# The second product of the second MLP's last 1536 tokens by seven block products, gates of a pass first

## The chip, the cores and the metric

The kernel runs on one core of a Trainium2 chip. The metric is device time in microseconds (us) of one execution, the median of several runs. One execution was also recorded by the hardware profiler; all rows below come from it. In the rows PE is the matmul engine TensorE, PEld its weight loads, DVE is VectorE, ACT is ScalarE, POOL is GpSimd, and SP is the engine that issues nearly all DMAs. L284 is line 284 of the kernel. A releaser is the instruction whose end let a waiting one start.

## What is computed

Random-feature attention over 4 batches of 576 tokens is followed by two MLPs over all 2304 tokens, in float32. Cut to what matters:

```
x = attention(q, k, v, omega)                 # 2304 tokens x 512
h = x @ w_in;   g = max(h, 0) + alpha * min(h, 0)
x = g @ w_out                                 # first MLP, 512 -> 2048 -> 512
h = x @ w_in2
g = where(h >= 1, h, where(h <= -1, 0, (h + 1) ** 2 / 4))
out = g @ w_out2                              # second MLP, 512 -> 2048 -> 512
```

## The kernel before

**Numbers as pairs.** Each float32 operand of an MLP product is held as a high part (rounded to the format that TensorE takes) and a low part (the rest). A product is three matmuls into the same sum: high by high, high by low, low by high (`mm3`, L284 to L286). Splitting an operand costs one ACT instruction for the high part (`hi_of`, L268) and one subtraction on DVE or POOL for the low part (`lo_of`, L277 to L279).

**Stages.** Attention and the first MLP's first three groups of 512 tokens run interleaved: 48 *units* (3 groups by 16 blocks of 128 hidden features). The first of them starts at about 56 us, the 48th ends at about 390 us. Then come four *passes* of 768 tokens: pass 0 is the rest of the first MLP, passes 1 to 3 are the whole second MLP. A pass has 8 *steps* (s = 8 p + j), and step j makes the hidden features of two blocks of 128.

**First product of a step.** It is done by seven block products instead of eight (Strassen's scheme in Winograd's form): input and weights are cut into 2 by 2 blocks, sums of blocks are made ahead, and product i (0 to 6) takes 6 matmuls of 128x384 (`product`). Products 4 and 6 are copied out by ACT (`kept_copy`, L1093) and products 2 and 3 are then added on top of them in the same PSUM bank (`CHAINS`). DVE forms four *corners* from the results (`shared_sum`, `added_corner`, `last_corner`: L1103, L1112, L943), each 128 features by 384 tokens. `corner` applies the gate (for the second MLP a clamp on DVE, a square on ACT, a maximum on DVE: L1143 to L1145) and splits the result into high and low part in one of four places (`out_g_slots`).

**Second product.** It is plain: per step two blocks by six rows of 128 tokens by three matmuls of 128x512, summed over the pass in six PSUM banks (`piece`). The pieces of step s - 1 are put between the seven products of step s by the list `PIECES`, so that DVE and ACT have a whole step of about 15.6 us to make one step's gates. At the end of a pass `store` copies six banks out and sends them to `out`.

**Weights.** The second MLP's weights come in while the first MLP and pass 0 run: `second_weights` starts block f at unit 16 + 3.4 f, `convert` turns the raw words into float32, `second_parts` makes and splits the block sums of the first product's weights, `keep_out` splits the second product's weights as they are. All go to DRAM through three staging tiles (`stage_slots`, tiles `w_keep`), and each step reloads them (`load_set`, `load_out`).

**Order.** The order of every engine is fixed when the kernel is built. `Plan` picks, one after the other, the stream that can start first by estimated durations, ranks and free places, so a changed stream also moves others. Every engine then works off its own list in order, and a wait holds up all that stands behind it.

Of the kernel before, what the change touches and what calls it, by code (L numbers as in the profile page):

```python
# [176 lines left out]
def favor_attention_two_mlps(  # L177
# [20 lines left out]
    nc = tc.nc  # L198
# [24 lines left out]
    W2S = 4, 5  # L223
    PACE = 34
# [134 lines left out]
    def keep_out(f, w):  # L359
        yield ev("w", 1, f, 1)  # L360
        j, u = divmod(f, 2)
        yield from keep(kept[1, j, 3 + u], w, (1, j, 3 + u))
        plan.put(w_slots[1], slot_of[1, f, 1])
# [534 lines left out]
    ORDER = [0, 5, 6, 3, 4, 1, 2]  # L898
    CHAINS = {2: 4, 3: 6}
# [8 lines left out]
    set_slots = [*part_slots, Tokens([0])]  # L908
# [6 lines left out]
    for m in range(2):  # L915
        for j in range(NJ2):
            for k in range(5):
                n = DM if k != 2 else 3 * DM // 2
                kept[m, j, k] = dram.tile([P, 2, n], F32, tag=f"kept{m}_{j}_{k}", name="w_kept")
    for j in range(NJ2):  # L920
        kept[0, j, 5] = dram.tile([P, 2, DM], F32, tag=f"odd{j}", name="w_kept")

# [77 lines left out]
    def load_set(s, k):  # L1000
        p, j, m = step(s)
        n = len(w_sets[k]) * DM // 2
        if s:
            yield ev("set", s - 1, k)
        if k < 2:
            yield ev("part", NU - 1, k)
        yield ev("second")
        yield ev("stored", m, j, k)
        if k == 2:
            yield ev("stored", m, j, 6)  # L1010
        t = yield set_slots[k]
        if k < 2:
            both = part_tile(t, "w_set")
        else:
            both = second[0].tile([P, 2, n], F32R, tag="w2", name="w_set")
        yield _dma(P * n * 8, lambda: nc.sync.dma_start(both.bitcast(F32), kept[m, j, k]))
        w_of[s, k] = both[:, 0, :], both[:, 1, :], t
        done("set", s, k)

    def load_out():  # L1020
        yield ev("g", NU - 1)
        for s in range(STEPS):
            p, j, m = step(s)
            for u in (1, 0):
                yield ev("stored", m, j, 3 + u)
                t = yield g_slots
                both = moe_p.tile([P, 2, DM], F32R, tag=t, name="w_out") if t[0] == "g" else part_tile(t, "w_out")
                out_of[s, u] = both[:, 0, :], both[:, 1, :], t
                plan.add(load(both.bitcast(F32), kept[m, j, 3 + u], ("out part", s, u)), 0)

    def inputs(p):
# [17 lines left out]
        engine = ("dve2",) if p else ("pool",)  # L1049
# [22 lines left out]
    def split_input(p, i, src):  # L1072
        yield x_slots[i]
        pool = second[0]
        hi = pool.tile([P, K2, GH], F32R, tag=f"sh{i}", name="x_hi")
        lo = pool.tile([P, K2, GH], F32R, tag=f"sl{i}", name="x_lo")
        yield hi_of(hi, src, 0)
        yield lo_of(lo, src, hi, ("dve2",) if p else ("pool",))
        x_of[p, i] = hi, lo
        done("xi", p, i)  # L1080
# [55 lines left out]

    def corner(s, q, h, key):
        p, j, m = step(s)
        u, half_ = divmod(q, 2)
        yield t_slots  # L1140
        t = temp("t")
        if m:
            yield _dve_fast(GH, lambda: nc.vector.tensor_scalar(t, h, -1.0, 1.0, ALU.max, ALU.min))  # L1143
            yield _act(GH, lambda: nc.scalar.activation(t, t, AF.Square, bias=half[:, 0:1], scale=0.5), 50)  # L1144
            yield _dve_two(GH, lambda: nc.vector.tensor_tensor(h, h, t, ALU.max))  # L1145
# [24 lines left out]
    def second_mlp():  # L1170
        yield ev("first hidden")
        banks = {}
        for s in range(STEPS + 1):
            pieces = second_project(s - 1) if s else iter(())
            p, j, _ = step(s)
            for i in range(2):
                done("unit", NU + 2 * s + i)
            for i, more in zip(ORDER, PIECES if s > NJ2 else FIRST_PIECES):
                if s < STEPS:
                    chain = CHAINS.get(i)  # L1180
                    k = place[i][0]
                    yield ev("set", s, k)
                    yield ev("xi", p, i)
                    if chain is None:
                        tag = yield h_banks
                        banks[i] = bank(tag), tag
                    else:
                        yield ev(f"e{chain}", s)
                        banks[i] = banks.pop(chain)
                    b, tag = banks[i] if i in (4, 6) else banks.pop(i)  # L1190
                    o = b[:, :GH]
                    yield product(s, i, o, chain is None)
                    if i in (0, 4, 6):
                        plan.add(kept_copy(s, f"e{i}", o, tag), URGENT)
                    if i == 5:
                        plan.add(shared_sum(s, o, tag), URGENT)
                        plan.add(last_corner(s), URGENT)
                        plan.add(shared_sum_used(s), URGENT)
                    if i in (1, 2, 3):
                        plan.add(added_corner(s, i - 1, o, tag), URGENT)  # L1200
                    if i == max(w_sets[k], key=ORDER.index):
                        plan.put(set_slots[k], w_of[s, k][2])
                    if j == NJ2 - 1:
                        plan.put(x_slots[i], 0)
                for _ in range(more):
                    yield from next(pieces, ())

    def spare():
        for j in range(NJ2):
            for k in (0, 1, 2, 3, 4, 6):  # L1210
                yield ev("kept", 1, j, k)
        i = yield stage_slots
# [48 lines left out]
    def piece(s, p, j, u, r):  # L1261
# [11 lines left out]
        yield _pe(mm3_ns(DM), lambda: mm3(y, gh, gl, hi, lo, first, last))  # L1273
        if last:
            plan.add(store(p - 1, r, y, tag, tokens), URGENT)
        if r % (NR // 2) == NR // 2 - 1:
            plan.put(out_g_slots[q], 0)
        if r == NR - 1:
            plan.put(g_slots, t_out)

    def store(p, r, y, tag, tokens):
# [18 lines left out]
        if c < B * SM:  # L1300
            b, t = divmod(c, SM)
            at = b * S + t
            yield _dma(P * DM * 4, lambda: nc.sync.dma_start(rows((at, at + P)), dst))
            return
        for i in range(P // SL):
            at = ((c - B * SM) // SL + i) * S + SM
            yield "dma", 300, lambda: nc.sync.dma_start(rows((at, at + SL)), dst[i * SL : (i + 1) * SL])

# [87 lines left out]
    for s in range(STEPS):  # L1396
        for k in range(3):
            plan.add(load_set(s, k), 0)
    for p in range(1 + NG):
        plan.add(inputs(p), URGENT + 1 + p)  # L1400
# [51 lines left out]
```

## Time and profile before

| | |
|---|---|
| median of 3 runs | 905.27 us (904.07 to 907.48) |
| profiled execution, its own time | 903.9 us |
| its span, first to last instruction | 902.1 us |
| PE busy | 887.8 us (98%) |
| DVE, ACT, POOL busy | 622.9, 457.9, 281.0 us |
| DMA moved | 221.36 MB, mean 245 GB/s |
| granted TensorE clock | 1.0 (2.4 GHz) in all 40 slices |

A busy figure is time in which an engine had work in flight. Matmuls overlap: the duration of one (391 ns for 128x512) is longer than the distance between the starts of two neighbours, and it is the distance that counts for the time of a long run of them. The span's stretches, cut at the first matmul of each pass, are: 145 to 390 us first MLP (with the attention's later part), then pass 0, 1, 2, 3.

### The profile page before, as it was taken

Reading aid. Unit: us, or ns where it says so; the run is one execution under the profiler, and the core shown is the slowest. Engines: PE = TensorE matmul, PEld = TensorE weight load, DVE = VectorE, ACT = ScalarE, POOL = GpSimd, SP = SyncE. Lnnn points to the kernel's source line nnn. Section 1 sums busy time; section 2 is a strip of 40 time slices with the busy share of each in tenths; the row PEclk is TensorE's granted clock in tenths of the full one; section 3 lists DMA queues with packets and bytes.
Section 4 is the critical chain, followed back from the end, with each engine's and each line's share of the span. In section 5 each row is a group of like instructions: output and inputs, shape, how many; then the busy total and the mean of one; then the engine's idle time right before and its main releaser. Section 6 shows DMA issues by size and latency. Waiting matters only on the chain.

```text
span 902.1 us, 16293 instructions
## 1 busy us (share of the span) xinstructions
PE 887.8 (98%) x6017; PEld 757.8 (84%) x6017; DVE 622.9 (69%) x1180; ACT 457.9 (51%) x998; POOL 281.0 (31%) x257
## 2 busy tenths in 40 slices
PE   8999999999999999999999999999999999999997
PEld 7677777777777788889999999999999989999996
DVE  5997767765556844597887999566855559565553
ACT  6886777555666422453444565343533335443333
POOL 1766666565758764931120022000000000000000
PEclk9999999999999999999999999999999999999999
DMA  8967765588988899989999879864665655664532
GB/s 215 240 198 226 209 232 191 175 266 297 312 298 290 293 326 344 330 322 322 308 340 323 291 263 321 289 207 167 216 240 187 198 172 202 223 213 158 206 111 94
DMA packets 84432, 221.36 MB, mean 245 GB/s; under 512 B 26752, under 2 KB 32512, under 8 KB 84352
## 3 DMA queue, kind: packets, MB, share of 16 engines
q1 hardware_dynamic: 84272, 220.27, 72.5%
q8 instruction: 48, 0.79, 0.3%
q14 instruction: 32, 0.26, 0.1%
q10 hardware_dynamic: 80, 0.03, 0.0%
HBM read 165.22 MB, written 55.05 MB: 244 GB/s over the span
## 4 chain that ended last, share of the span: by engine, by line
PE 89%; DVE 3%; DMA 2%; ACT 2%; issue 1%; POOL 1%; SPq 1%; DVEq 0%; POOLq 0%; ACTq 0%
PE h L284 13%; PE h L286 13%; PE h L285 13%; PE y L284 11%; PE y L285 11%; PE y L286 11%; PE a L286 3%; PE a L285 3%; PE a L284 3%; PE a L602 2%; PE a L465 2%; PE a L539 1%; PE a L568 1%; DMA w_set<-w_kept 1%; DVE nm L432 1%
## 5 line engine op out<-in xcount | busy, mean ns | idle before, releaser
L284 PE MATMUL h<-x_hi,w_set 128*128 128x384 f32 x448 | 151.4, 338 | 0.8 <-DMA w_set<-w_kept 0.5
L286 PE MATMUL h<-x_hi,w_set 128*128 128x384 f32 x448 | 150.9, 337 | 0.0
L285 PE MATMUL h<-x_lo,w_set 128*128 128x384 f32 x448 | 150.6, 336 | 0.0
L327 POOL TENSOR_TENSOR w<-w,raw 128x512 uint32<-128x512 uint32 x64 | 90.0, 1414 | 188.3 <-DVE w L326 143.2
L1144 ACT ACTIVATE t<-t,half 128x384 f32<-128x384 f32 x96 | 58.9, 613 | 91.5 <-DVE t L1143 91.1
L284 PEld LDWEIGHTS h<-x_hi,w_set 128*128 128x128 f32 x448 | 84.2, 188 | 9.4 <-DVE w_keep L278 0.9
L285 PEld LDWEIGHTS h<-x_lo,w_set 128*128 128x128 f32 x448 | 84.1, 188 | 7.5
L268 ACT ACTIVATE g<-c 128x384 fp32r<-128x384 f32 x96 | 50.4, 525 | 67.8 <-DVE c L1145 36.3
L286 PEld LDWEIGHTS h<-x_hi,w_set 128*128 128x128 f32 x448 | 84.1, 188 | 0.0
L284 PE MATMUL y<-g,w_parts 128*128 128x512 f32 x192 | 78.2, 407 | 0.6 <-ACT kf L443 0.6
L284 PE MATMUL h<-x_hi,w_parts 128*128 128x512 f32 x192 | 78.7, 410 | 0.0
L286 PE MATMUL h<-x_hi,w_parts 128*128 128x512 f32 x192 | 75.4, 393 | 0.9 <-POOL w_parts L279 0.8
L1093 ACT COPY e<-h 128x384 f32<-128x384 f32 x96 | 45.4, 473 | 59.2 <-PE h L286 58.4
L286 PE MATMUL y<-w_out,g 128*128 128x512 f32 x192 | 75.3, 392 | 0.0
L284 PE MATMUL y<-w_out,g 128*128 128x512 f32 x192 | 75.2, 392 | 0.0
L285 PE MATMUL y<-w_out,g 128*128 128x512 f32 x192 | 75.1, 391 | 0.0
L285 PE MATMUL y<-g,w_parts 128*128 128x512 f32 x192 | 75.1, 391 | 0.0
L286 PE MATMUL y<-g,w_parts 128*128 128x512 f32 x192 | 75.0, 391 | 0.0
L285 PE MATMUL h<-x_lo,w_parts 128*128 128x512 f32 x192 | 75.0, 391 | 0.0
L279 POOL TENSOR_TENSOR w_parts<-w,w_parts 128x512 fp32r<-128x512 f32 x48 | 62.8, 1316 | 34.3 <-ACT w_parts L268 27.9
L278 DVE TENSOR_TENSOR g<-c,g 128x384 fp32r<-128x384 f32 x96 | 54.6, 568 | 21.6 <-ACT g L268 21.3
L812 DVE TENSOR_SCALAR t<-h,alpha_sb 128x512 f32<-128x512 f32 x48 | 35.9, 748 | 47.1 <-PE h L286 47.0
(167 smaller groups left out, 2011.9 us busy)
## 6 DMA issues: line engine op xcount, KB each, us to landing
w_set<-w_kept SPq DMA_DIRECT2D x64, 512.0 KB, 4.6
w_out<-w_kept SPq DMA_DIRECT2D x64, 512.0 KB, 5.0
w_kept<-w_keep SPq DMA_DIRECT2D x56, 512.0 KB, 6.2
raw<-w SPq DMA_DIRECT2D x48, 512.0 KB, 5.9
w_parts<-w_kept SPq DMA_DIRECT2D x48, 512.0 KB, 5.3
w_set<-w_kept SPq DMA_DIRECT2D x32, 768.0 KB, 4.4
w_kept<-w_parts SPq DMA_DIRECT2D x32, 512.0 KB, 4.3
kq<-kq SPq DMA_DIRECT2D x15, 576.0 KB, 5.5
```

Of the source, the lines that this page charges most:

```text
L268: ops = [_act(n, lambda: nc.scalar.activation(hi, src, AF.Copy))]
L278: "dve2": _dve_two(n, lambda: nc.vector.tensor_tensor(*args), bias),
L279: "pool": _pool(n, lambda: nc.gpsimd.tensor_tensor(*args)),
L284: nc.tensor.matmul(out_, wh, mh, start=first, stop=False, skip_group_check=more)
L285: nc.tensor.matmul(out_, wh, ml, start=False, stop=False, skip_group_check=more)
L286: nc.tensor.matmul(out_, wl, mh, start=False, stop=last, skip_group_check=more)
L327: yield _pool(n, lambda: nc.gpsimd.tensor_tensor(d, d, low, ALU.add))
L465: nc.tensor.matmul(o, x[rows, c], om[rows, :], start=True, stop=True)
L602: nc.tensor.matmul(o[r], weights[i], moving[i], start=True, stop=True)
L812: yield _dve(SM + 57, lambda: nc.vector.tensor_scalar(t, h, 0.0, a, ALU.min, ALU.mult))
L1093: yield _act(GH, lambda: nc.scalar.copy(e, src))
L1144: yield _act(GH, lambda: nc.scalar.activation(t, t, AF.Square, bias=half[:, 0:1], scale=0.5), 50)
```

## The change

For passes 2 and 3 (steps from `PLAIN` = 16 on) the second product is also done by seven block products. Each pass is put into two halves: first all eight steps of the first product with all their gates, kept as 32 float32 tiles in SBUF places that have fallen free (`open_units`), then 7 by 8 block products (`second_products`) of 9 matmuls of 128x256, one product index after the other, each summed over the eight j in two banks. The token-side block sums are made by `gate_sums` on DVE or POOL, the operands are split by `operands`, up to four ahead, and `out_sums` forms the output corners. The weight-side sums are made once by `out_parts`, eight blocks per pair of f, so twice the bytes go to DRAM; `second_weights` starts at unit 12. The gate of passes 1 to 3 becomes two ACT instructions and one on DVE. Loads of passes 2 and 3 go through one ring of tiles (`late_loads`), and the first product's order in steps after 16 is `LATER_ORDER`. Pass 0 and pass 1 keep the plain second product.

```diff
-            yield ev("unit", NF + PACE * f // 10)
+            yield ev("unit", W2_FROM + PACE * f // 10)
...
-            if a:
-                plan.add(keep_out(f, w), NU + f)
...
+            if a and f % 2:
+                plan.add(out_parts(f // 2), NU + f)
+
+    def out_parts(j):
...
+        yield either(h, "tensor_tensor", (t1, b12, b11, ALU.subtract), off_way())
+        yield either(h, "tensor_tensor", (t2, b22, t1, ALU.subtract), off_way())
+        plan.add(keep_halves(sa.rearrange("p a n -> p (a n)"), ((j, 4), (j, 5))), rank)
+        yield either(h, "tensor_tensor", (t3, b22, b12, ALU.subtract), off_way())
+        yield either(h, "tensor_tensor", (t4, b21, t2, ALU.subtract), off_way())
+        plan.add(keep_halves(sb.rearrange("p a n -> p (a n)"), ((j, 6), (j, 3))), rank)
...
+    def keep_halves(src, keys):
+        i = yield stage_slots
...
+        yield hi_of(hi, src, 600)
+        yield lo_of(lo, src, hi, off_way())
...
+    LATER_ORDER = [0, 6, 4, 5, 3, 2, 1]
+    OUT_ORDER = [0, 4, 5, 6, 2, 3, 1]
+    OUT_CHAINS = {2: 4, 3: 6, 1: 0}
+    PLAIN = 2 * (NF // 2)
...
-        engine = ("dve2",) if p else ("pool",)
+        engine = ("dve2",) if p else ("dve2", "pool")
...
+    def gate(t, h, to):
+        yield _act(GH, lambda: nc.scalar.activation(t, h, AF.Relu, bias=half[:, 0:1], scale=0.5), 90)
+        yield _act(GH, lambda: nc.scalar.activation(t, t, AF.Square))
+        yield _dve_two(GH, lambda: nc.vector.scalar_tensor_tensor(to, h, 1.0, t, ALU.max, ALU.min))
...
+            if j == 0 and p > 2:
+                yield from second_products(p - 1)
+            pieces = second_project(s - 1) if 0 < s <= PLAIN else iter(())
...
+            order = ORDER if s <= PLAIN else LATER_ORDER
+            more = [0] * 7 if s > PLAIN else PIECES if s > NJ2 else FIRST_PIECES
...
+        yield from second_products(NG)
...
+        yield either(GH, "tensor_tensor", (a21, a21, a22, ALU.add), both)
+        done("first sum", s)
...
+    def operand(p, i, j, slot):
...
+        yield hi_of(hi, src)
+        yield lo_of(lo, src, hi, ("dve2",))
...
+                def products():
+                    for c, o in enumerate(os):
+                        r = slice(c * P, (c + 1) * P)
+                        mm3(o, hi[:, r], lo[:, r], w_hi, w_lo, chain is None and j == 0 and c != 1, j == NJ2 - 1, True)
```

On TensorE in a step of pass 2 or 3, before: `h` is a first product, `y` a sum of the second product, `g` the gates as weights, `w_out` the streamed weights.

```order
L285 MATMUL y_7725<-w_out,g_4276 128x512
L286 MATMUL y_7725<-w_out,g_4276 128x512
L284 MATMUL h_8540<-x_hi,w_set 128x384
L285 MATMUL h_8540<-x_lo,w_set 128x384
L286 MATMUL h_8540<-x_hi,w_set 128x384
```

After, at the end of the gates of pass 3, where the last first product meets the first block product:

```order
L286 MATMUL h_9874<-x_lo,w_set 128x384
L287 MATMUL h_9874<-x_hi,w_set 128x384
L285 MATMUL a_9885<-w_out,g_4352 128x256
L286 MATMUL a_9885<-w_out,g_4352 128x256
L287 MATMUL a_9885<-w_out,g_4352 128x256
```

Pieces of 128x512 no longer stand between the first products: 42 first-product matmuls per step follow each other in the gate half, and 504 of 128x256 in the product half.

On DVE in one step of pass 3, before (`u`, `e`, `c` are the sums that make the corners, `t` the gate's clamp, `g` the low parts):

```order
L1103 TENSOR_TENSOR u<-h_9091,e_9090 128x384
L278 TENSOR_TENSOR g_4275<-c_9067,g_4275 128x384
L943 TENSOR_TENSOR e_9122<-e_9122,u 128x384
L1112 TENSOR_TENSOR c_9141<-h_9115,u 128x384
L1143 TENSOR_SCALAR t<-c_9141 128x384
L1145 TENSOR_TENSOR c_9141<-c_9141,t 128x384
L278 TENSOR_TENSOR g_4276<-c_9141,g_4276 128x384
```

After, the first whole step of pass 3 (`gates` and `x` are places of kept gates, L995 a sum of them):

```order
L1236 TENSOR_TENSOR u<-y_9259,e_9237 128x384
L995 TENSOR_TENSOR e_9248<-e_9248,u 128x384
L1245 TENSOR_TENSOR c_9279<-y_9238,u 128x384
L995 TENSOR_TENSOR e_9248<-e_9248,e_9258 128x384
L1245 TENSOR_TENSOR c_9288<-a_9249,u 128x384
L1245 TENSOR_TENSOR c_9301<-y_9289,e_9237 128x384
L1273 SCALAR_TENSOR_TENSOR gates<-c_9279,gates 128x384
L1273 SCALAR_TENSOR_TENSOR gates<-e_9248,gates 128x384
L1273 SCALAR_TENSOR_TENSOR gates<-c_9288,gates 128x384
L995 TENSOR_TENSOR gates<-gates 128x384
L1273 SCALAR_TENSOR_TENSOR gates<-c_9301,gates 128x384
L995 TENSOR_TENSOR x<-gates 128x384
```

These 12 instructions are the whole step; before, a step had 18. The low parts (L279) have moved behind the last gate of the pass, two of the four sums per step as well. From one `u` to the next DVE has 12 to 14 instructions in the gate halves, ACT 11 to 13 (three copies, eight for the gates, at times a high part).

On POOL near the end of its list, before (`w` is a converted weight, `w_keep` a low part on its way to DRAM):

```order
L279 TENSOR_TENSOR x_lo<-x,x_hi 128x768 x2
L327 TENSOR_TENSOR w<-w,raw 128x512
L279 TENSOR_TENSOR w_keep<-w,w_keep 128x512
L327 TENSOR_TENSOR w<-w,raw 128x512 x20
```

After, where its conversions of the second MLP's weights near their end:

```order
L328 TENSOR_TENSOR w<-w,raw 128x512 x4
L996 TENSOR_TENSOR w_sum<-w 128x256
L996 TENSOR_TENSOR w_sum<-w,w_sum 128x256
L280 TENSOR_TENSOR w_keep<-w,w_keep 128x2x256 x2
L280 TENSOR_TENSOR w_keep<-w_sum,w_keep 128x2x256
L996 TENSOR_TENSOR w_sum<-w 128x256
```

POOL takes sums and low parts of the second product's weights between the conversions, and gives the eleven sums and low parts of pass 0's input (`x_lo`, `x_sum`, `x`, 128x768) to DVE. Over its whole list it gains 23 sums of 128x256 and 13 low parts of 128x512. ACT gains 15 high parts of 128x512 for these weights (one more is on DVE), and the stores of this product's weights to DRAM change from 16 of 512 KB to 64 of 256 KB.

## Rows read from the trace of the kernel before

**Rows 1.** The page's first part: busy us, share of span, instructions.

```profile
span 902.1 us, 16293 instructions
PE 887.8 (98%) x6017; PEld 757.8 (84%) x6017; DVE 622.9 (69%) x1180; ACT 457.9 (51%) x998; POOL 281.0 (31%) x257
```

**Rows 2.** Waits of PE, longest first: us in total, times, longest.

```profile
PE a L602 <- ACT kf L443: 1.7, 1, 1.7
```

**Rows 3.** Stretches: length; busy PE, PEld, DVE, ACT, POOL (x); clock, DMA share, GB/s.

```profile
145.00:390.00 245.00, 241.76 (x1792) 189.70 (x1792) 149.70 (x248) 124.80 (x283) 163.70 (x151) 1.00 0.84 287
390.00:514.20 124.20, 123.44 (x697) 114.04 (x696) 107.04 (x207) 57.40 (x109) 18.79 (x13) 1.00 0.92 322
514.20:638.90 124.70, 124.70 (x638) 113.31 (x637) 97.67 (x194) 59.49 (x114) 12.65 (x7) 1.00 0.71 249
638.90:763.80 124.90, 124.90 (x626) 112.91 (x625) 80.33 (x160) 50.74 (x98) 0.00 (x0) 1.00 0.57 198
763.80:902.10 138.30, 133.24 (x661) 119.34 (x659) 74.45 (x153) 53.49 (x104) 0.00 (x0) 1.00 0.50 169
```

**Rows 4.** Timeline of PE at the start of pass 2: start us, us, instruction.

```profile
638.88 0.34 PE L284 MATMUL h<-x_hi,w_set 128*128 128x384 f32 x1
...
640.99 0.39 PE L284 MATMUL y<-w_out,g 128*128 128x512 f32 x1
...
643.40 0.39 PE L284 MATMUL y<-w_out,g 128*128 128x512 f32 x1
...
645.45 0.34 PE L284 MATMUL h<-x_hi,w_set 128*128 128x384 f32 x1
```

**Rows 5.** Timeline of PE in pass 0: three matmuls of 128x256, and what follows.

```profile
450.95 0.27 PE L284 MATMUL a<-g,w_out 128*128 128x256 f32 x1
451.06 0.28 PE L285 MATMUL a<-g,w_out 128*128 128x256 f32 x1
...
451.30 0.34 PE L284 MATMUL h<-x_hi,w_set 128*128 128x384 f32 x1
```

**Rows 6.** Timeline of PE and PEld: twelve filling matmuls of 128x256 at 50 us.

```profile
49.97 1.69 PE L1337 MATMUL h<-warm_w 128*128 128x256 f32 x12
49.97 1.48 PEld L1337 LDWEIGHTS h<-warm_w 128*128 128x128 f32 x12
```

**Rows 7.** Timeline of DVE: two instructions back to back at 640 us.

```profile
639.43 0.56 DVE L278 TENSOR_TENSOR g<-e,g 128x384 fp32r<-128x384 f32 x1
639.90 0.56 DVE L1145 TENSOR_TENSOR c<-c,t 128x384 f32<-128x384 f32 x1
```

**Rows 8.** Groups of ACT instructions by line: count, busy us, mean ns, idle before.

```profile
L1144 ACT ACTIVATE t<-t,half 128x384 f32<-128x384 f32 x96 | 58.9, 613 | 91.5 <-DVE t L1143 91.1
L1093 ACT COPY e<-h 128x384 f32<-128x384 f32 x96 | 45.4, 473 | 59.2 <-PE h L286 58.4 <-ACT x L844 0.8
L268 ACT ACTIVATE w_keep<-w_sum 128x512 fp32r<-128x512 f32 x32 | 19.9, 630 | 16.9 <-DMA w_kept<-w_keep 11.6 <-POOL w_sum L944 4.1 <-DVE w_sum L943 1.3
```

**Rows 9.** Groups of POOL and DVE instructions on the weights' sums.

```profile
L279 POOL TENSOR_TENSOR w_keep<-w_sum,w_keep 128x512 fp32r<-128x512 f32 x22 | 28.4, 1299 | 9.4 <-ACT w_keep L268 9.0
L944 POOL TENSOR_TENSOR w_sum<-w 128x256 f32<-128x256 f32 x22 | 16.6, 756 | 0.3
L943 DVE TENSOR_TENSOR w_sum<-w 128x256 f32<-128x256 f32 x10 | 6.4, 641 | 1.4 <-POOL w L327 1.4
L943 DVE TENSOR_TENSOR w_sum<-w_sum,w 128x256 f32<-128x256 f32 x5 | 2.1, 418 | 0.0
```

**Rows 10.** Who waited for the stores of kept weights (L997): us, times.

```profile
  ACT w_keep L268: 17.1, 12
```

**Rows 11.** The end of the span: last matmul, last copies, last DMA issues.

```profile
896.66 0.39 PE L286 MATMUL a<-w_out,g 128*128 128x512 f32 x1
896.40 1.26 ACT L1290 COPY x<-a 128x512 f32<-128x512 f32 x2
897.01 2.52 SPq L1307 DMA_DIRECT2D out<-x  x4
```

More of the change, by code (lines that the diff above doesn't have):

```diff
@@ L916, in favor_attention_two_mlps @@
         for j in range(NJ2):
-            for k in range(5):
+            for k in range(3 if m else 5):
                 n = DM if k != 2 else 3 * DM // 2
@@ L1172, in second_mlp @@
         banks = {}
-        for s in range(STEPS + 1):
-            pieces = second_project(s - 1) if s else iter(())
+        for s in range(STEPS):
             p, j, _ = step(s)
+            if j == 0 and p > 2:
+                yield from second_products(p - 1)
+            pieces = second_project(s - 1) if 0 < s <= PLAIN else iter(())
             for i in range(2):
                 done("unit", NU + 2 * s + i)
[L1178 to L1205, printed above, removed]
-                    yield from next(pieces, ())
@@ new lines, in second_mlp, with gate_sums @@
+        yield from second_products(NG)
+    tiles_of_set = ["w00", "w01"], ["w10", "w11", "extra"]
+    def gate_sums(s):
+        p, j, _ = step(s)
+        for q in range(4):
+            yield ev("unit space", j, q)
+        a11, a21, a12, a22 = (units_of[j, q] for q in range(4))
+        at = (p - 1) * GT + j % 2 * GH
+        s2 = x_all[:, j // 2, at : at + GH]
+        both = "dve2", "pool"
+        for q in (1, 3):
+            yield ev("gate", s, q)
+        yield either(GH, "tensor_tensor", (a21, a21, a22, ALU.add), both)
+        done("first sum", s)
+        yield ev("gate", s, 0)
+        yield either(GH, "tensor_tensor", (s2, a21, a11, ALU.subtract), both)
+        done("second sum", s)
+        yield ev("gate", s, 2)
+        yield ev("split", s, 4)
+        yield either(GH, "tensor_tensor", (a21, a12, s2, ALU.subtract), both)
+        done("fourth sum", s)
+        yield ev("split", s, 0)
+        yield either(GH, "tensor_tensor", (a11, a22, s2, ALU.subtract), both)
+        done("third sum", s)
@@ new lines, in operands @@
+    def operands(p):
+        n = 0
+        for i in OUT_ORDER:
+            for j in range(NJ2):
+                yield out_g_slots[n % 4]
+                plan.add(operand(p, i, j, n % 4), URGENT)
+                n += 1
+    SOURCES = {
+        4: ("first sum", 1),
+        0: (None, 0),
+        5: ("second sum", None),
+        6: ("third sum", 0),
+        2: ("fourth sum", 1),
+        3: ("third sum", 3),
+        1: ("fourth sum", 2),
+    }
+    def operand(p, i, j, slot):
+        s = p * NJ2 + j
+        key, q = SOURCES[i]
+        yield from (ev("gate", s, 0),) if i == 0 else (ev(key, s),)
+        at = (p - 1) * GT + j % 2 * GH
+        src = x_all[:, j // 2, at : at + GH] if q is None else units_of[j, q]
+        hi, lo = (late["g", slot // 2][:, a, slot % 2 * GH : (slot % 2 + 1) * GH] for a in range(2))
+        yield hi_of(hi, src)
+        yield lo_of(lo, src, hi, ("dve2",))
+        done("split", s, i)
+        operand_of[s, i] = hi, lo
+        if i in (6, 2, 3, 1):
+            plan.put(unit_slots[j, q], 0)
@@ new lines, in favor_attention_two_mlps, with shares_used, send @@
+    shared = {}
+    def shares_used(p):
+        yield ev("last sum", p)
+        for key in ("e4", "c1"):
+            plan.put(temp_slots[key], 0)
+        for i in (2, 3):
+            yield ev("read out", p, i)
+        for key in ("u", "c2"):
+            plan.put(temp_slots[key], 0)
+    def send(c, src, cols):
+        if c < B * SM:
+            b, t = divmod(c, SM)
+            at = b * S + t
+            yield _dma(P * src.free_size() * 4, lambda: nc.sync.dma_start(out[at : at + P, cols], src))
+            return
+        for i in range(P // SL):
+            at = ((c - B * SM) // SL + i) * S + SM
+            yield "dma", 300, lambda: nc.sync.dma_start(out[at : at + SL, cols], src[i * SL : (i + 1) * SL])
```

285 lines of the change are left out of this document (263 added, 22 removed).

## The prediction

> **What bounds the kernel now.** I read the busy shares first: PE has work in flight for 887.8 of 902.1 us, and no other engine comes near [rows 1]. A busy PE can still be a PE that waits inside, so the waits come next: the longest single wait of PE in the whole execution is 1.7 us [rows 2]. The stretches say where the rest stands: in the first MLP PE is idle for 245 - 241.76 = 3.2 us, in pass 0 for 0.8 us, in passes 1 and 2 not at all, and the 5.1 us of the last stretch lie behind the last matmul [rows 3, 11]. So TensorE's own instruction stream sets the time, and a change pays by what it takes out of that stream, less the waits it puts in. The granted clock is 1.00 throughout [rows 3], that is 2.4 GHz, and PE stays busy, so I let it stand.
>
> The length of a matmul in the stream is the distance between two starts, not its duration. Pass 2 shows both kinds: 12 matmuls of 128x384 from 638.88 to 640.99, 2.11 / 12 = 0.176 us each; 9 of 128x512 from 643.40 to 645.45, 2.05 / 9 = 0.228 us each [rows 4]. A pass has 8 x 42 = 336 of the first and 8 x 36 = 288 of the second: 336 x 0.176 + 288 x 0.228 = 59.1 + 65.6 = 124.7 us, and the stretch of pass 2 is 124.9 us long [rows 3]. The budget closes.
>
> **Second product, on the path.** Removed per pass: 288 x 0.228 = 65.6 us. Added: 7 x 8 x 9 = 504 matmuls of 128x256. Pass 0 has such matmuls, in threes: 450.95 to 451.30, 0.117 us each [rows 5]. They stand between wider ones there, and each has its own weight load, so a long run could be slower. The longest run in the trace is twelve: their loads take 1.48 us in all, 0.123 each with the last one's full duration counted in, and by the matmuls' modelled ends 1.69 / 12 = 0.141 [rows 6]. These are the bounds; I take 0.117, because the last duration is what inflates the other two. 504 x 0.117 = 59.0 us, so 6.6 to 6.8 us are saved per pass, 13.5 us in two (by 0.123: 3.6 per pass, 7.2 in two). The first product keeps its 336 matmuls.
>
> **Gate halves.** Fifteen steps now run without pieces between the products: 42 x 0.176 = 7.4 us per step, where a step had 15.6. DVE has 12 to 14 instructions per step there. Back to back they start 0.47 us apart, with a duration of 0.56 [rows 7]: 5.6 to 6.6 us if they overlap as in the row, 6.7 to 7.8 if none does. Only the two steps with 14 could exceed 7.4. Pass 0 already runs DVE at 107.04 of 124.2 us, 86%, with PE idle for 0.8 us [rows 3], and 13 x 0.47 is 83%. ACT has three copies and eight gate instructions: 3 x 0.473 + 8 x 0.613 = 6.3 us [rows 8], with one high part 6.9. The place to watch is product 3: it is added on top of product 6, so PE may start it only when ACT has copied product 6, and two products, 2 x 6 x 0.176 = 2.1 us, stand between. One copy takes 0.47, so ACT may be late by some 1.6 us, less than three of its instructions. I take 0 here and keep 15 x 0.4 = 6 us as the upper end.
>
> **Product halves.** A block product lasts 9 x 0.117 = 1.05 us, and four operands may be ready ahead. A place that falls free has to be refilled within three products, 3.15 us, by a high part on ACT (0.61 by the longest row of that shape) and a low part on DVE (0.56): 1.2 us, which leaves room for one foreign instruction on each. What is tight is DVE's sum. Between the 8th and the 24th low part of pass 2 the new order has 36 DVE instructions, because the third and fourth token sums have to be made there. 16 products last 16.8 us; 36 x 0.47 = 16.9 us, 36 x 0.56 = 20.2 us. Behind it come the input sums of pass 3 in the same pass. So a loss of 0 to 3.4 us per pass; nearer to the overlapped row, I take 1.5 us for both passes together.
>
> **The ends of a half.** The first four operands are split steps earlier, and eight banks are there for two that the first block product wants, so PE goes straight on: 0. Behind the last product ACT copies 512 and 256 columns, and SP issues three DMAs where two of the last four waited for the last copy: four issues took 2.52 us, 0.63 each [rows 11], so three after a copy end where they ended before. Tail 0, give or take 0.5.
>
> **The weights, up to pass 1.** Added: 23 sums and 13 low parts on POOL, 23 x 0.756 + 13 x 1.299 = 34.3 us [rows 9]; 15 high parts of 0.63 on ACT, 9.5 us, and in pass 1 some 32 more gate instructions of at most 0.613, 19.6 us [rows 8]. From 145 us to the end of pass 1 POOL is busy for 195 of 494 us, ACT for 59.5 of the 124.7 us of pass 1 [rows 3], so this lies beside PE's work. 8.4 MB more go to DRAM. If all fell into 145 to 390 us, 287 GB/s would become (70.3 + 8.4) / 245 = 321 GB/s, which pass 0 holds now at a DMA share of 0.92. Starting at unit 12 puts part of it ahead. The loads of passes 2 and 3 grow by 6.3 MB each, to some 263 GB/s, below pass 0 too. The three staging tiles are the narrow place: ACT stood 17.1 us in 12 waits for stores [rows 10]; staging is used 64 times instead of 48, which by proportion makes 22.8 us, 5.7 more. While an ACT or POOL instruction waits, gate copies queue behind it, and PE behind those. Of the old 17.1 us at most 4.0 can have reached PE, the idle time of these stretches; I take 0.5 us, bounds -2 (the old idle time shrinks, as the order there is shuffled) and 5.7.
>
> POOL and DVE also meet: DVE's `w_sum` took 0.641 us where its left-over form took 0.418, while POOL was at work beside it [rows 9]. At 0.22 us for each of the 36 added POOL instructions that is 8 us on DVE over 494 us, where DVE has over 130 us free.
>
> **Sum.** 903.9 - 13.5 + 1.5 + 0.5 = 892.4 us for an execution like the profiled one. That one was 1.4 us below the median of the runs (905.27), so as a median 893.8 us.
>
> **Rivals.**
> *A, DVE sets the pace in passes 2 and 3.* If nothing overlaps, the product halves lose 2 x 3.4 and the gate halves up to 6: 893.8 - 1.5 + 12.8 = 905.1 us, no change. For it: 36 instructions in 16.8 us. Against it: pass 0 at 86%, and the 0.47 of the row. Chance 0.10, mostly with half of the loss (about 899).
> *B, the weights' preparation reaches PE.* 5.7 us instead of 0.5: 899.0 us. For it: DMA at 0.92 and ACT waiting for stores. Against: those waits hardly reached PE before. Chance 0.12.
> *C, weight loads set the pace of 504 narrow matmuls in a row; slower.* It decides from 65.6 / 504 = 0.130 us per matmul. At 0.141, the upper bound, a pass gets 71.1 - 65.6 = 5.5 us longer: 903.9 + 11 + 2 + 1.4 = 918.3 us. For it: PEld is busy for 84% of the span [rows 1]. Against it: three and twelve in a row at 0.117 to 0.123. Chance 0.05.
> The Trainium skill's "TensorE: Matmul & The Clock Gate", section "Back-to-back issue gap", speaks for C: it gives sustained 81 ns at 128 columns and 131 ns at 512, with the weight load in it, so that a straight line makes a half-wide matmul cost 98 / 131 = 0.75 of a wide one (an estimate from that page). By it a pass would grow by 20 us and the time would be near 946 us. The trace does not agree: 0.117 / 0.228 = 0.51 [rows 4, 5].
>
> **How the numbers follow.** Forecast, 890 to 898 us: 0.70. B 0.12, A 0.10, C 0.05, and 0.03 for a wait that I have not seen and that costs over 10 us. Half a per cent of 905.27, 4.5 us, is about what a measurement can tell from no change: faster means below 900.7. Forecast, most of B and half of A are faster: 0.85; the rest of A and B is the same, 0.09; C and the unseen wait are slower, 0.06. The range takes in B and half of A: 889 to 902 us.
>
> **What would show it.** Right: pass 3's gate half 8 x 7.4 = 59 us and its product half 59 us long, with starts of 128x256 matmuls 0.117 us apart and next to no PE waits. A shows as PE waiting for DVE's `g` in the product halves, or for ACT's `e` before product 3. B shows as idle PE before 639 us. C shows as distances above 0.12 with no releaser. The forecast is wrong if PE's waits in passes 2 and 3 add up to more than 6 us.

## The result and the profile after

The changed kernel takes 891.4 us (median of 4 runs, 890.52 to 893.54); the kernel before took 906.01 us beside it (904.07 to 907.48). The ratio is 0.9843, 95% interval 0.9816 to 0.987. The forecast was 893.8 us in a range of 889 to 902, so the time is in the range, 2.4 us below the forecast.

The page's first part of the kernel after, against [rows 1]: PE has 432 matmuls more and is busy 10.4 us less.

```profile
span 889.2 us, 17834 instructions
PE 877.4 (99%) x6449; PEld 770.7 (87%) x6449; DVE 685.4 (77%) x1239; ACT 528.9 (59%) x1160; POOL 301.1 (34%) x284
```

The stretches of the kernel after, in the columns of [rows 3]: length, busy time and count of PE, PEld, DVE, ACT and POOL, granted clock, DMA share, GB/s. Passes 2 and 3 are each cut at the point where the gates end and the block products begin (706.2 and 825).

```profile
145.00:390.00 245.00, 243.36 (x1796) 191.00 (x1795) 165.36 (x269) 128.14 (x292) 145.72 (x141) 0.95 0.86 296
390.00:514.20 124.20, 123.04 (x697) 114.08 (x696) 106.43 (x190) 58.30 (x108) 34.53 (x27) 0.95 0.92 320
514.20:639.10 124.90, 124.70 (x637) 113.04 (x636) 104.69 (x176) 83.64 (x162) 33.53 (x28) 0.95 0.90 306
639.10:706.20 67.10, 67.10 (x374) 65.35 (x373) 55.91 (x105) 41.97 (x90) 2.21 (x2) 0.95 0.73 250
706.20:766.40 60.20, 60.20 (x506) 60.20 (x505) 50.15 (x100) 33.62 (x66) 0.00 (x0) 0.95 0.85 278
766.40:825.00 58.60, 58.60 (x339) 58.60 (x338) 46.19 (x93) 39.41 (x88) 0.00 (x0) 0.95 0.66 228
825.00:885.30 60.30, 60.30 (x505) 60.10 (x504) 43.67 (x87) 31.91 (x64) 0.00 (x0) 0.95 0.66 212
```

The clock of 0.95 in this one record had no effect that I can find: the kernel without the late sums (below), recorded at 1.00, has the same distances between matmuls in these stretches (0.1745 us at 384 columns, 0.1195 at 256). I take both as the 2.4 GHz level.

Pass 0 starts at 389.69 us (before 389.91), pass 1 at 513.96 (514.12), pass 2 at 639.03 (638.88). So up to pass 2 the two traces differ by 0.15 us. From the start of pass 2 to the start of the last matmul it was 638.88 to 896.66, 257.8 us; now it is 639.03 to 885.03, 246.0 us. That is 11.8 us less. From the start of the last matmul to the end, 5.47 us have become 4.22, 1.25 us less. 11.8 + 1.25 - 0.15 = 12.9 us, the whole difference of the spans.

All waits of PE that the trace names from 389 us to the end, in total 1.4 us and all of them ahead of pass 2 (waited for, us in total, times, longest):

```profile
PE h L285 <- ACT e L1226: 0.7, 2, 0.5
PE h L285 <- DVE c L1245: 0.7, 1, 0.7
```

The timeline of PE where pass 2's gates end, and up to 26 us later (start us, duration, instruction):

```profile
705.79 0.34 PE L286 MATMUL y<-x_lo,w_set 128*128 128x384 f32 x1
705.97 0.34 PE L287 MATMUL y<-x_hi,w_set 128*128 128x384 f32 x1
706.14 0.28 PE L285 MATMUL h<-w_out,g 128*128 128x256 f32 x1
706.26 0.28 PE L286 MATMUL h<-w_out,g 128*128 128x256 f32 x1
...
707.44 0.28 PE L287 MATMUL h<-w_out,g 128*128 128x256 f32 x1
...
729.80 0.28 PE L285 MATMUL a<-w_out,g 128*128 128x256 f32 x1
...
732.32 0.28 PE L285 MATMUL y<-w_out,g 128*128 128x256 f32 x1
```

There is no gap at the seam: 0.17 us from the last wide matmul to the first narrow one. The first eleven distances are 1.30 / 11 = 0.118 us each, the 21 from 729.80 to 732.32 are 2.52 / 21 = 0.120.

### The profile page after: what moved, and what is told of

Same layout as the page of the kernel before. It is cut to its first block, busy times and chain, and to the rows that moved or that the text cites. A ratio compares the mean times of both kernels' runs of the same rounds, so it can differ in the third digit from the quotient of the medians.

```text
span 889.2 us, 17834 instructions
## 1 busy us (share of the span) xinstructions
PE 877.4 (99%) x6449; PEld 770.7 (87%) x6449; DVE 685.4 (77%) x1239; ACT 528.9 (59%) x1160; POOL 301.1 (34%) x284
## 4 chain that ended last, share of the span: by engine, by line
PE 85%; DVE 5%; DMA 4%; ACT 2%; issue 2%; POOL 1%; SPq 1%; ACTq 0%; DVEq 0%; POOLq 0%
PE y L285 11%; PE y L286 11%; PE y L287 11%; PE h L285 11%; PE h L287 10%; PE h L286 10%; PE a L287 4%; PE a L286 4%; PE a L285 4%; DMA raw<-w 3%; PE a L504 2%; PE a L641 2%; PE a L578 1%; PE a L607 1%; DMA kq<-kq 1%
## 5 line engine op out<-in xcount | busy, mean ns | idle before, releaser
L328 POOL TENSOR_TENSOR w<-w,raw 128x512 uint32<-128x512 uint32 x64 | 87.9, 1380 | 183.5 <-DVE w L327 169.6
L285 PE MATMUL h<-x_hi,w_set 128*128 128x384 f32 x288 | 97.4, 338 | 1.4 <-ACT e L1226 0.7
L287 PE MATMUL h<-x_hi,w_set 128*128 128x384 f32 x288 | 97.0, 337 | 0.0
L286 PE MATMUL h<-x_lo,w_set 128*128 128x384 f32 x288 | 96.9, 336 | 0.0
L285 PE MATMUL y<-w_out,g 128*128 128x256 f32 (+1 forms) x192 | 61.3, 319 | 0.0
L286 PE MATMUL y<-w_out,g 128*128 128x256 f32 (+1 forms) x192 | 61.1, 318 | 0.0
L287 PE MATMUL y<-w_out,g 128*128 128x256 f32 (+1 forms) x192 | 61.1, 318 | 0.0
L285 PEld LDWEIGHTS h<-x_hi,w_set 128*128 128x128 f32 x288 | 54.2, 188 | 6.2 <-ACT e L1226 1.5
L286 PEld LDWEIGHTS h<-x_lo,w_set 128*128 128x128 f32 x288 | 54.1, 188 | 3.5
L269 ACT ACTIVATE g<-gates 128x384 fp32r<-128x384 f32 x72 | 37.6, 525 | 31.8 <-PE y L286 22.1
L269 ACT ACTIVATE g<-h 128x512 fp32r<-128x512 f32 x48 | 28.8, 601 | 44.6 <-DVE h L852 44.4
L316 ACT ACTIVATE raw<-raw 128x512 f32<-128x512 f32 x55 | 37.4, 679 | 30.3 <-DMA raw<-w 30.0
L287 PEld LDWEIGHTS h<-x_hi,w_set 128*128 128x128 f32 x288 | 54.1, 188 | 0.0
L280 POOL TENSOR_TENSOR w_keep<-w_sum,w_keep 128x512 fp32r<-128x512 f32 x32 | 42.3, 1328 | 33.7 <-ACT w_keep L269 33.3
```

The costliest lines, as they stand in the source:

```text
L269: ops = [_act(n, lambda: nc.scalar.activation(hi, src, AF.Copy))]
L280: "pool": _pool(n, lambda: nc.gpsimd.tensor_tensor(*args)),
L285: nc.tensor.matmul(out_, wh, mh, start=first, stop=False, skip_group_check=more)
L286: nc.tensor.matmul(out_, wh, ml, start=False, stop=False, skip_group_check=more)
L287: nc.tensor.matmul(out_, wl, mh, start=False, stop=last, skip_group_check=more)
L316: _act(n, lambda: nc.scalar.activation(f, f, AF.Copy, scale=2.0**-112), 45),
```

## Experiments: which part of the change does what

Ratios are to the kernel before, run in the same series. Stretches are compared from the start of pass 0 on: ahead of it, executions differ by several us among themselves, whatever the change (unit 12 begins at 144.7 to 152.3 us in the traces). A kernel given with one run has no interval. Beside the old order, the two doublings and the constant weights the kernel before ran only once too, 909.39 us, so there the traces decide.

**The preparation alone.** The plain second product stays in all passes; the sums of its weights are still made, split and stored, but not used.

```diff
-    PLAIN = 2 * (NF // 2)
+    PLAIN = 4 * (NF // 2)
...
-        for p in range(2, 1 + NG):
+        for p in range(PLAIN // NJ2, 1 + NG):
...
-            if j == 0 and p > 2:
-                yield from second_products(p - 1)
...
-        yield from second_products(NG)
```

> Only the preparation: all the added block sums, splits and stores of the second product's weights, the start at unit 12 and the new form of the gate, but the second product of all passes plain as before. Theory: the preparation and the gate's form cost nothing, 905 to 907.5 us beside 906.0 before. Rival B: 909 to 912 us, and then the block products would have gained that much more than they show.

Measured: 904.43 us (902.47 to 906.75, 10 runs), ratio 0.9969 (0.9955 to 0.9983), 2.8 us faster than the kernel before, which took 907.17 us in this series; no gain was expected. Its stretches from 145 us, pass 0, 1 and 2:

```profile
145.00:390.00 245.00, 243.45 (x1800) 191.16 (x1799) 167.12 (x271) 130.90 (x300) 151.39 (x144) 1.00 0.86 295
393.00:516.70 123.70, 122.85 (x697) 114.24 (x696) 105.59 (x191) 58.30 (x108) 36.47 (x27) 1.00 0.93 321
516.70:641.80 125.10, 124.91 (x638) 113.21 (x638) 104.70 (x176) 83.34 (x162) 33.54 (x28) 1.00 0.89 307
641.80:766.60 124.80, 124.80 (x626) 112.81 (x625) 71.25 (x129) 66.48 (x128) 0.00 (x0) 1.00 0.60 198
```

From pass 0 to the end it takes 512.00 us, the kernel before 512.22. The preparation costs nothing that can be seen there, so the 2.8 us should lie ahead of pass 0. The trace itself does not show them: its execution was the slowest of the ten and reached pass 0 3.1 us later than the kernel before.

**The preparation alone, started at unit 16.** One candidate for the 2.8 us is the earlier start, which puts the instructions around 206 us in another order.

```diff
-    W2_FROM = 12
+    W2_FROM = 16
```

> All the added preparation of weights, the new gate and the new order of loads, but plain second products in all passes, and the preparation started at unit 16 as in the kernel before (the run of this kind with the start at unit 12 was 2.8 us faster than the kernel before). Theory, the gain came from the start at unit 12, which shuffles the order around 206 us so that the 1.7 us wait of PE for ACT's copy vanishes: 906 to 908 us, ratio 0.999 to 1.002, with that wait back. Rival, the gain has nothing to do with the start (shorter gate, other loads): 903.5 to 905 us, ratio about 0.997.

Measured: 908.2 us (904.43 to 912.98, 12 runs), ratio 1.0024 (1.0005 to 1.0043), with a wait of PE for `kf` around 206 us back, as in [rows 2]:

```profile
PE a L641 <- ACT kf L482: 1.3, 1, 1.3
```

With the start at unit 12 the preparation is a small gain, at unit 16 a loss of up to 0.4%. The gap of 0.55% is 5 us, more than this wait alone; the rest I cannot place.

**The whole change, started at unit 16.** The same edit on the changed kernel.

> The changed kernel with the second MLP's weights started at unit 16 again instead of 12. Theory (the preparation of the weights lies beside TensorE's work, and the early start only spreads it): within 1.5 us of the changed kernel's 891.4 us, PE waits before pass 2 below 5 us in all. Rival B (the preparation reaches PE, and the early start is what keeps it off): 5 us or more slower, with PE waiting for DMA, ACT or POOL in passes 0 and 1.

Measured: 892.64 us (891.29 to 896.38), ratio 0.9849 (0.9822 to 0.9877). The wait is there too:

```profile
PE a L641 <- ACT kf L482: 2.0, 1, 2.0
```

Here the start makes no difference that the runs can tell. The two pairs, 0.55% and 0.06%, hardly fit each other. The traces agree on a part: between 145 and 390 us PE is idle for 3.2 us in each of the three kernels that start at unit 16 (the kernel before among them), and for 1.4 to 2.4 us in each of the eleven that start at unit 12. So the early start is worth 1 to 2 us there; what it is worth in all stays open between nothing and some 5 us.

**Pass 3 alone by block products.** Pass 2 stays plain; the loads follow the same number.

```diff
-    PLAIN = 2 * (NF // 2)
+    PLAIN = 3 * (NF // 2)
```

> The changed kernel with block products in pass 3 alone (pass 2 plain). Theory (each pass saves what TensorE's columns save, 65.6 - 60.2 = 5.4 us, and the shorter tail of 1.2 us belongs to the last pass): 906.0 - 5.4 - 1.2 = 899.4, so 898 to 900.5 us. If the two passes gained through something shared (the end of the kernel, the preparation), it is off the middle: near 892 or near 905 us.

Measured: 896.23 us (895.13 to 899.38), ratio 0.9888 (0.9864 to 0.9913). It lies below the expected time, by about the 2.8 us that the preparation alone gained. From the start of pass 3 to the last matmul it takes 127.24 us (765.99 to 893.23), where the preparation alone took 132.93: 5.7 us less, and the tail is 1.1 us shorter. One pass therefore gives about half of the gain, as the forecast's sum by passes has it.

**The first product's order.** The old order in the steps after 16, where product 3 follows product 6 at once.

```diff
-    LATER_ORDER = [0, 6, 4, 5, 3, 2, 1]
+    LATER_ORDER = [0, 5, 6, 3, 4, 1, 2]
```

> The changed kernel with the old order of the first products in the gate halves (0, 5, 6, 3, 4, 1, 2), so that product 3 stands right behind product 6, on whose copied-out bank it is added, instead of two products later. Theory (PE then waits in each of the 15 steps for 0.2 us until the result is there and 0.47 us of ACT's copy): 15 x 0.7 = 10 us more, 899 to 905 us, with the wait of h for ACT's e at the head of PE's list. Rival A (ACT is late there anyway): 15 us or more. If ACT had been no concern at all: no change.

Measured: one run of 905.07 us, 13.7 us above the changed kernel. PE's waits from 639 us on, one in each of the 15 steps:

```profile
PE h L285 <- ACT e L1226: 3.4, 6, 0.6
PE y L285 <- ACT e L1226: 2.8, 5, 0.6
PE a L285 <- ACT e L1226: 2.3, 4, 0.6
```

The gate half of pass 3 takes 65.33 us (773.70 to 839.02) instead of 58.6, 0.84 per step; from pass 2 to the end it is 262.6 us, 12.4 more than in the changed kernel and only 0.6 less than in the kernel before. PE now waits for ACT's copies. So with the old order the block products would have given next to nothing: without pieces of the second product between the first products, the copy has to be covered by two other products, and the new order does that.

**DVE's margin in the gate halves.** Each gate's last instruction is done twice, four more per step.

```diff
             yield from gate(t, h, t)
+            yield _dve_two(GH, lambda: nc.vector.scalar_tensor_tensor(t, h, 1.0, t, ALU.max, ALU.min))
```

> The changed kernel with the last instruction of each gate in passes 2 and 3 done twice on DVE (same result): 4 more DVE instructions per step, 16 to 18 instead of 12 to 14. DVE is busy for 46.2 us with 93 instructions in the 58.6 us of pass 3's gate half. Theory (the gate halves have about 1.5 us of DVE room per step): 16.5 x 0.50 = 8.2 us per step against 7.35, 0.9 x 15 = 13 us more, 897 to 907 us; at 0.47 per instruction 6 us. Rival (PE is held by ACT's copies, not by DVE): below 2 us.

Measured: one run of 902.42 us. Pass 3's gate half takes 64.63 us (771.44 to 836.07), 0.75 more per step. The longest waits of PE:

```profile
PE y L285 <- ACT e L1226: 6.0, 5, 2.5
PE a L285 <- ACT e L1226: 0.7, 1, 0.7
```

The releaser is ACT, though only DVE was given more: ACT's gate instructions wait for DVE's corners, and the copies queue behind them. By throughput alone 16 x 0.47 = 7.5 us on DVE would have been 0.2 us over a step of 7.33. DVE is not full either: it is busy for 57.2 of the 64.7 us. So the waits come from the chain through both engines, which has less margin than the busy shares say; that is argued from these waits, and no run takes the chain apart.

**DVE's margin in the product halves.** Each low part is subtracted twice, 56 more instructions per half.

```diff
         yield lo_of(lo, src, hi, ("dve2",))
+        yield lo_of(lo, src, hi, ("dve2",))
```

> The changed kernel with every low part of a block product's operand subtracted twice on DVE: 56 more DVE instructions of 128x384 in each product half. DVE is busy there for 50.2 and 43.7 of 60 us with 100 and 87 instructions. Theory (DVE has only the rest of the 60 us to spare): at 0.50 us per instruction 78 and 72 us are wanted, so 18 and 12 us more, 30 us in all, 911 to 923 us, the waits on DVE's g. If DVE had far more room than its busy time says: below 900 us.

Measured: one run of 915.77 us; the halves take 72.1 and 69.3 us instead of 60.2. PE's longest waits:

```profile
PE h L287 <- DVE g L279: 3.6, 6, 1.2
PE y L287 <- DVE g L279: 2.8, 2, 1.6
PE h L285 <- ACT g L269: 2.1, 1, 2.1
PE y L285 <- ACT g L269: 2.1, 1, 2.1
```

This is rival A, forced. DVE is busy for 71.0 us of the first half and for 65.4 of the second, with 147 and 139 instructions. In the first that is 72.1 / 147 = 0.49 us each: those of 128x384 that follow each other at once start 0.47 us apart, as in [rows 7], and some wider ones raise the mean. The expectation's 0.50 was about right; its halves of 78 and 72 us were too long because it counted 156 and 143 instructions in them. At 0.49 us a half of 60.2 us has room for some 120; the change has 100 and 87.

## Experiments: why the narrow matmuls stand 0.1195 us apart

A product half takes 60.2 us where 59.0 was forecast. With no wait in it, that is a longer distance: 60.2 / 504 = 0.1195 us.

**No late sums.** The third and fourth token sums are left out, some of DVE's work in the product halves.

```diff
         yield ev("split", s, 4)
-        yield either(GH, "tensor_tensor", (a21, a12, s2, ALU.subtract), both)
         done("fourth sum", s)
         yield ev("split", s, 0)
-        yield either(GH, "tensor_tensor", (a11, a22, s2, ALU.subtract), both)
         done("third sum", s)
```

> The changed kernel without the third and fourth token sum of each step (32 instructions on DVE or POOL in passes 2 and 3 together are left out; the products take the gates unsummed instead). They stand mostly in the product halves. Theory (TensorE sets the pace there, 0.1195 us per matmul of 128x256): 890.5 to 892 us, distance unchanged. Rival A (DVE feeds the products too slowly, and 0.1195 instead of 0.117 is its trace): distance 0.117, 2 to 3 us faster.

Measured: 891.96 us (890.13 to 895.66), ratio 0.984 (0.9811 to 0.987); the halves last as long as in the changed kernel, 0.1195 us per matmul, with 82 and 73 instructions on DVE instead of 100 and 87. So DVE's load has no part in it.

**A constant in place of the weights.**

```diff
-                w_hi, w_lo = (both[:, j % 2, a, :] for a in range(2))
+                w_hi, w_lo = (late["zero"][:, a * h : (a + 1) * h] for a in range(2))
```

> The changed kernel with the streamed operand of every block product read from one constant tile of zeros instead of the tiles that the weights were loaded to (the loads stay; the output is not the product). In the changed kernel's product halves the distance is 0.118 us for the products that read some of the eight tiles and 0.120 for the others. If the place of the streamed operand in SBUF sets it: one distance throughout, near 0.118 or near 0.120. If it is the weights, the sums or DMA traffic: the same mixture, 0.1195 on average. The time moves by less than 2 us in either case.

Measured: one run of 894.22 us. One distance throughout: 0.120 in 494 of the first half's 503 distances. Its timeline in the first product half:

```profile
729.77 0.28 PE L286 MATMUL a<-zero,g 128*128 128x256 f32 x1
...
732.29 0.28 PE L286 MATMUL y<-zero,g 128*128 128x256 f32 x1
```

21 distances in 2.52 us. In the changed kernel six of the eight tiles that hold streamed weights show 0.120 as well, and two show 0.118. With one tile for all, the mixture is gone, though the loads went on. So it hangs on the streamed tile and not on the loads; the numbers became one constant too, so this run alone does not rule them out. In the program as built, the six tiles and the operands (which are loaded as TensorE's weights) all lie at bytes divisible by 128 in a partition, the other two lie 96 bytes past such a place. Three kernels shift one or the other and keep the numbers.

```diff
+    parts_p.tile([P, 8], F32, tag="pad", name="pad")
```

> The changed kernel with 32 unused bytes put ahead of one set of SBUF tiles, so that all eight tiles of streamed second-product weights and the tiles of split operands lie at byte places that are 32 modulo 64. So far the block products that stream a tile at 0 modulo 64 start 0.120 us apart (six of eight tiles), those at 32 modulo 64 start 0.118 apart (two tiles), and the operands lie at 0. Theory, the streamed tile's own place counts: 0.118 in all 1008 block-product matmuls, product halves of 59.6 us instead of 60.2, 890.2 us against 891.4 (a difference no run of three rounds can tell, so the trace decides). Rival, the streamed tile's place relative to the operand's counts (0.120 where they agree, 0.118 where they differ): 0.120 in all, product halves of 60.4 us, 891.8 us. Rival, it is neither and another property of the two tiles: unchanged, six tiles at 0.120 and two at 0.118.

```diff
+        late["pool"].tile([P, 8], F32, name="pad")
```

> The changed kernel with 32 unused bytes put ahead of the tiles of split operands alone: these move from 0 to 32 modulo 64, the streamed tiles stay (six at 0, two at 32). Theory, the streamed tile's own place counts: six tiles at 0.120 and two at 0.118 as in the changed kernel. Rival, the relative place counts: reversed, six tiles at 0.118 and two at 0.120, product halves of 59.7 us. Total within 1 us of 891.4 by either.

```diff
+        late["pool"].tile([P, 16], F32, name="pad")
```

> The changed kernel with 64 unused bytes ahead of the tiles of split operands alone. So far, by the difference of the two places (streamed tile less operand) modulo 128: 0 gave 0.1192 to 0.1194 us per block-product matmul (two kernels), 32 or 96 gave 0.117 to 0.118, and 64 gave 0.114 to 0.116, but 64 was only seen at the same two of the eight streamed tiles. Now the other six tiles are at 64 and those two at 32. Theory, the difference modulo 128 sets the distance: 0.114 to 0.116 at the six tiles, product halves of 0.75 x 504 x 0.115 + 0.25 x 504 x 0.118 = 58.3 us instead of 60.2, some 3.8 us less in both, 887.6 us where the changed kernel has 891.4 (ratio to the kernel before about 0.980). Rival, 0.114 to 0.116 belongs to those two tiles and not to the difference: 0.118 to 0.120 at the six tiles, halves of 59.5 to 60.2 us, 890 to 891.5 us.

Measured, as distances inside a tile in the first and second product half (us), by the streamed tile's place less the operand's, modulo 128 (0.113 is where the distance settles a few matmuls into a tile; with these first ones the mean of the two tiles is 0.1145):

| kernel | six tiles | two tiles | the halves, us |
|---|---|---|---|
| changed kernel | 0: 0.120, 0.120 | 96: 0.118, 0.118 | 60.2, 60.2 |
| 32 bytes ahead of weights and operands | 0: 0.120, 0.120 | 64: 0.113, 0.113 | 59.75, 59.5 |
| 32 bytes ahead of the operands | 96: 0.118, 0.118 | 64: 0.113, 0.118 | 59.2, 59.5 |
| 64 bytes ahead of the operands | 64: 0.113, 0.118 | 32: 0.117, 0.119 | 57.8, 59.5 |

Times: 891.63 us (888.01 to 896.91), ratio 0.9834 (0.9808 to 0.986); one run of 892.17; 889.91 us (887.98 to 894.21), ratio 0.9825 (0.9793 to 0.9858). The last kernel's timeline, first in pass 2's product half, then in pass 3's:

```profile
729.81 0.28 PE L285 MATMUL a<-w_out,g 128*128 128x256 f32 x1
...
732.30 0.28 PE L286 MATMUL y<-w_out,g 128*128 128x256 f32 x1
...
849.82 0.28 PE L287 MATMUL y<-w_out,g 128*128 128x256 f32 x1
...
852.30 0.28 PE L287 MATMUL h<-w_out,g 128*128 128x256 f32 x1
```

22 distances in 2.49 us are 0.113 each, 21 in 2.48 us are 0.118. The theory I began with, the streamed tile's own place, is refuted: six tiles moved from 0 to 32 kept 0.120, since the operands moved along. The relation of the two places counts: at 0 it was 0.120 every time, at 32 and 96 it was 0.117 to 0.119, at 64 it was 0.113 in four halves and 0.118 in two. Why it fell short in those two, both of them pass 3's, stays open.

The last kernel is the fastest, but its interval overlaps the changed kernel's, so it is not shown to be faster. Its halves are 3.1 us shorter in all (expected 3.8). Part is given back: pass 1 takes 126.6 us (514.77 to 641.36) instead of 125.1: its operands lie in the moved tiles too, and its 128x512 matmuls went from 0.227 to 0.234 us. For the wide ones the equal place is the better one. The kernel before shows it as well: its 128x512 matmuls with a streamed `w_out` tile stand 0.227 us apart where that tile lies at the operand's place, and 0.233 where it lies 96 bytes off.

## Why the prediction was right, term by term

**The second product, -13.5 us: right in kind, 2.7 us too much.** It was 2 x (65.6 - 60.2) = 10.8 us, since a half takes 60.2 us where 59.0 was counted. The step that was mis-sized is the choice of 0.117 from three matmuls in pass 0 [rows 5]; the truth, 0.1195, lay between it and the bound of 0.123 [rows 6]. A check stood in [rows 4]: a straight line through 0.176 at 384 columns and 0.228 at 512 gives 0.124 at 256, 0.0045 too high where 0.117 was 0.0025 too low; the two enclose what was measured. Rival C's slower kernel is out: the distance never reached 0.130, though PEld is busy for all of the 60.2 us. Whether the weight loads have a share in the 0.1195 is not shown. The rule of the Trainium skill, "TensorE: Matmul & The Clock Gate", section "Back-to-back issue gap", by which the time was estimated near 946 us, is not borne out: half the columns cost 0.1195 / 0.228 = 0.52 of the distance, not 0.75.

**Gate halves, 0: right.** Pass 3's takes 58.6 us; 8 x 7.4 = 59.2 was forecast; 336 x 0.1745 = 58.6, and the trace names no wait of PE in it. The forecast named the copy of product 6 as the place to watch and took two products as enough cover. The old order, with no product between, shows the cost of having none: 12.4 us. The margin was small: four more DVE instructions per step cost 0.75 us per step, more than the 0.4 of the upper end.

**Product halves, +1.5 us: it was 0.** DVE has 100 instructions in the first half and is busy for 50.15 of 60.2 us, where some 120 would fit; no low part came late. The forecast's count was right: from the 8th to the 24th low part DVE has 36 instructions, and they take 16.7 us. But the 16 products take 17.2 instead of 16.8 us, as the distance is longer. It was close: the sixth low part of pass 2 ended 0.24 us before the first matmul that reads it.

**Tail, 0: it was -1.25 us.** The end of the span, after:

```profile
884.99 0.58 ACT L1461 COPY x<-a 128x512 f32<-128x512 f32 x1 [3.52 <-PE a L287]
885.03 0.28 PE L287 MATMUL y<-w_out,g 128*128 128x256 f32 x1
885.47 0.38 ACT L1461 COPY x<-y 128x256 f32<-128x256 f32 x1
885.60 1.31 SPq L1531 DMA_DIRECT2D out<-x  x3
```

The 512-wide copy starts ahead of the last matmul, since its bank is complete three matmuls earlier. Only the narrow copy comes behind the last one, and three issues take 1.31 us, 0.44 each; the forecast had taken 0.63 each from four issues that lasted 2.52 us [rows 11] and saw only the count, not the earlier first copy. It also took issues of another kind: those four send 64 rows each (L1307), these three 128 rows, like L1303 before, one of which took 0.33 us.

**Weights, +0.5 us: right where the trace can tell.** From 145 to 390 us PE is idle for 245 - 243.36 = 1.6 us instead of 3.2, in pass 0 for 1.2 instead of 0.8. ACT's waits for the stores grew as forecast, even beyond 22.8 us:

```profile
ACT w_keep L269 <- DMA w_kept<-w_keep: 27.9, 24, 2.9
```

Next to nothing of it reached PE: from pass 0 on PE waited 0.7 us for ACT's copies, and ahead of it PE was idle less than before. Rival B is out. DMA in pass 1 rose from 249 to 306 GB/s, near the level that pass 0 held already. Over all runs the preparation alone was 2.8 us faster than before, below the term and also below its lower bound of -2. By the traces 1 to 2 us of it are idle time of PE ahead of pass 0 that the earlier start took away; where the rest comes from stays open, as the two kernels that start at unit 16 don't agree.

**The sum.** Against the forecast the second product gave 2.7 us less, the waits in the product halves 1.5 us more, the tail 1.25, the part up to pass 2 another 0.35 (0.15 us lost instead of 0.5), and the 672 first products some 1.0, as they stand 0.1745 us apart where 0.176 was read: 2.7 - 1.5 - 1.25 - 0.35 - 1.0 = -1.4. The profiled execution was forecast at 892.4 us and came out at 891.07. So errors of up to 2.7 us cancelled in part, and that the sum came this close is luck. The other 1 us of the 2.4 is the step from one execution to the median: the profiled one lay 1.4 us under the median before and 0.3 us under it after. By the experiments' medians and traces the change is -2.8 for the preparation, twice -5.7 for a pass and -1.1 for the tail, -15.3 us, near the -14.6 measured; so in the medians the weights' term is nearer -2.8 than +0.5. The chances had a slip: C and the unseen wait add up to 0.08, not 0.06.

## What to carry to other kernels

Where TensorE is busy throughout, leaving out one multiplication in eight pays most of its share (here 5.4 of 65.6 / 8 = 8.2 us per pass, the rest lost to narrower matmuls that cost more per column), if the elementwise work that it adds fits under the matmuls that are left. When wide filler matmuls are taken out from between dependent ones, order the rest so that every copy has other products to cover it: the order alone was worth 12.4 us, nearly as much as the whole change. Read the distance of a new matmul shape from two neighbouring shapes in long runs as well as from the one short run that has it: here the two estimates enclosed the measured one.

## What was unexpected of the hardware

The distance of 128x256 matmuls depends on where the streamed tile lies relative to the tile of the operand that is loaded as weights: 0.120 us at the same place modulo 128 bytes, 0.117 to 0.119 at 32 or 96 bytes off, 0.113 in four of six cases at 64 off (0.118 in the other two). At 512 columns it was the other way, 0.227 at the same place and 0.233 to 0.234 at 96 or 64 bytes off. The Trainium skill, "TensorE: Matmul & The Clock Gate", section "Step-by-step: what each phase is for", says that loading the next weights takes no read bandwidth from the running matmul; these runs show that the places of the two operands matter to each other, but neither by which mechanism nor whether the load is the cause.

DVE at saturation started an instruction of 128x384 every 0.47 us, though each has a duration of 0.55: the sum of the durations overstates what DVE needs. And the first 150 us differ by several us from one execution to the next, so that 2 or 3 us of a whole kernel cannot be placed there from single traces.
